# K in 8 KB pieces with the heads on alternate partitions, in a grouped-query attention kernel

## The chip, the cores and the metric

The kernel runs on one core of a Trainium2 chip. The metric is the device time of one execution in microseconds (us). The runs shown before the change have a median of 355.04 us (three runs, 353.94 to 355.42). The engines are named as in the profile: PE (matmuls; PEld are its weight loads), DVE (vector engine), ACT (activations), POOL, and SP, whose queue issues all transfers of this kernel.

## The reference

```python
B, Hq, Hkv, Sq, Sk, D = 16, 32, 8, 16, 2048, 128      # all bf16, normal * 0.05
k = jnp.repeat(k, Hq // Hkv, axis=1)
v = jnp.repeat(v, Hq // Hkv, axis=1)
scores = jnp.einsum("bhqd,bhkd->bhqk", q, k) * D ** -0.5
p = jax.nn.softmax(scores, axis=-1)
return jnp.einsum("bhqk,bhkd->bhqd", p, v)
```

There are 16 x 8 = 128 heads of K and V, each 2,048 keys of 128 values (512 KB). Four query heads of 16 rows share one of them, so each head of K meets 64 rows of Q.

## The kernel before

**Pairs.** Two heads of K (g = 0 and 1) make a pair p, and there are 64 pairs. Their 2 x 64 query rows fill the 128 partitions of S, P and O.

**Transfers (SP).** `load_k` (L143 to L151) brings the pair's K into one of six buffers `Kn`, `load_v` (L158) V into one of eight buffers `Vb`, `load_q` (L165) the Q of eight pairs, `store` (L170) a pair's output. SP's loop runs over t: K of pair t, Q when due, V of pair t - 4, the output of pair t - 17. A K load waits until the transposes of the pair that held its buffer are done, a V load until that pair's PV is done, a store until its output is written. In K and V of a head, partition a holds the 16 keys 16a to 16a + 15, 4 KB in one piece; a transfer of a pair thus has 256 pieces of 4 KB. The K of pair 0 comes as two transfers, one for each head, with a semaphore each.

**DVE.** For each pair it runs, in this order: the maximum of pair p (L281), the reciprocal of the row sums of pair p - 1 (L272), and the two transposes of K for pair p + 2 (L265). The transposes, one for each head, regard K as fp32 words (two bf16 side by side) and transpose blocks of 32 x 32 words, so that afterwards the partitions 32r to 32r + 31 hold the 32 words of a half of d, for the keys of row group r. The maximum reads the pair's 2,048 scores of S from PSUM, multiplies them by minus the scale, writes them to `Sneg` in SBUF as fp32 and takes the minimum along each row (`nbias`).

**PE.** Its order is written out in a list: S of pair p + 1 (L221), PV of pair p - 2 (L247), a part of the next Q's transposes if due (L204), the transposes of P of pair p (L236, in two halves of four). S has one buffer in PSUM, so S of the next pair waits for the maximum of this one. S of a pair is 32 matmuls, each over 32 partitions and 512 keys: four accumulations (the halves b of d and the two bf16 e of a word), four row groups r, two heads g. The moving operand is K, read one bf16 out of each fp32 word, with a step of 4 bytes:

```python
kt = KT[p % NKT][:, :, :].bitcast(BF16).rearrange("p g (t b x e) -> p g b e t x", t=J // 2, b=2, e=2)
```

**ACT.** It takes the exponential of `Sneg` into P (L310, with the row sums), copies the transposed P out of PSUM (L320), copies the transposed Q out of PSUM with a step of 128 bf16 in its input (L300), and scales the output of PV (L330). The exponential writes P in an order in which, after the transposes of P, the keys stand on the partitions on which V has them.

Of the kernel before, what the change touches and what calls it, by code (L numbers as in the profile page):

```python
# [7 lines left out]
BF16 = mybir.dt.bfloat16  # L8
F32 = mybir.dt.float32
I32 = mybir.dt.int32  # L10

NK = 6
NV = 8
NKT = 3
# [10 lines left out]
def bass_standalone__gqa_softmax__sampling_kernel(  # L25
# [11 lines left out]
    NP = G // 2  # L37
    J = Sk // 128
    assert J == 16 and NP % 8 == 0
    NQC = NP // 8  # L40
    scale = float(D) ** -0.5
# [5 lines left out]
    iota_t = sb("iota_t", [128, 128], I32)  # L47
    ident = sb("ident", [128, 128], BF16)
    ident4 = sb("ident4", [128, 128], F32)
    Kn = [sb(f"Kn{i}", [128, 2, J * 128], BF16) for i in range(NK)]  # L50
    Vb = [sb(f"Vb{i}", [128, 2, J, 128], BF16) for i in range(NV)]

    KT = [sb(f"KT{i}", [128, 2, J * 64], F32) for i in range(NKT)]
    Qn = [sb(f"Qn{i}", [128, 8, 128], BF16) for i in range(NQ)]

    QT = [sb(f"QT{i}", [128, 4, 1024], BF16) for i in range(2)]
# [27 lines left out]

    qf = q.rearrange("b h s d -> (b h s) d")
    of = out.rearrange("b h s d -> (b h s) d")
    kf = k.rearrange("b h s d -> (b h) (s d)").rearrange("g (a x) -> a g x", a=128)
    vf = v.rearrange("b h s d -> (b h) (s d)").rearrange("g (a x) -> a g x", a=128)  # L90


# [39 lines left out]
    with nc.Block() as block:  # L132
# [8 lines left out]
        @block.sync  # L141
        def _(sp):
            def load_k(p):  # L143
                s = p % NK
                if p >= NK:
                    sp.wait_ge(sem_kt, 2 * (p - NK) + 2)
                if p == 0:
                    for g in range(2):
                        sp.dma_start(Kn[s][:, g, :], kf[:, g, :]).then_inc(sem_k0[g], 16)  # L149
                else:  # L150
                    sp.dma_start(Kn[s][:, :, :], kf[:, 2 * p:2 * p + 2, :]).then_inc(sem_k[s], 16)  # L151

            def load_v(p):
                s = p % NV
                if p >= NV:
                    sp.wait_ge(sem_pv, p - NV + 1)
                dst = Vb[s][:, :, :, :].rearrange("a g j d -> a g (j d)")
                sp.dma_start(dst, vf[:, 2 * p:2 * p + 2, :]).then_inc(sem_v[s], 16)  # L158

            def load_q(c):  # L160
                s = c % NQ
                if c >= NQ:
                    sp.wait_ge(sem_st, last_q[c - NQ, 3] + 1)
                src = qf[1024 * c:1024 * (c + 1), :].rearrange("(a j) d -> a j d", j=8)
                sp.dma_start(Qn[s][:, :, :], src).then_inc(sem_q[s], 16)  # L165

            def store(p):
                s = p % NO
                sp.wait_ge(sem_nm, p + 1)
                sp.dma_start(of[128 * p:128 * (p + 1), :], Osb[s][:, :]).then_inc(sem_o[s], 16)  # L170

            for t in range(NP + SLAG + 1):
                if t < NP:
                    load_k(t)
                for c in range(NQC):
                    if t == max(0, 8 * c - QLEAD):
                        load_q(c)
                if 0 <= t - VLAG < NP:
                    load_v(t - VLAG)
                if 0 <= t - SLAG < NP:  # L180
                    store(t - SLAG)
            for s in range(NO):
                sp.wait_ge(sem_o[s], 16 * len(range(s, NP, NO)))

        @block.tensor
        def _(pe):
            pe.wait_ge(sem_id, 3)

            def free(u):
                if u >= NSTAGE:  # L190
                    pe.wait_ge(sem_ev, u - NSTAGE + 1)

            for op in pe_prog:
                if op[0] == "QT":
                    _, c, i, u = op
                    if i == 0:
                        pe.wait_ge(sem_q[c % NQ], 16 * (c // NQ + 1))
                    free(u)
                    dst = stage_ap(u).bitcast(BF16)
                    src = Qn[c % NQ][:, :, :].rearrange("p j (b c e) -> p j b e c", b=2, e=2)  # L200
                    b, e = divmod(i, 2)
                    for j in range(8):
                        for r in range(4):
                            ins = pe.transpose(dst[32 * r:32 * (r + 1), 128 * j:128 * (j + 1)], src[:, j, b, e, :], ident[:, :])  # L204
                    ins.then_inc(sem_st, 1)
                elif op[0] == "S":
                    _, p = op
                    pe.wait_ge(sem_kt, 2 * p + 2)
                    if p >= 1:
                        pe.wait_ge(sem_max, p)  # L210
                    c, i = divmod(p, 8)
                    if i == 0:
                        pe.wait_ge(sem_ev, last_q[c, 3] + 1)
                    kt = KT[p % NKT][:, :, :].bitcast(BF16).rearrange("p g (t b x e) -> p g b e t x", t=J // 2, b=2, e=2)
                    qt = QT[c % 2]
                    for acc in range(4):
                        b, e = divmod(acc, 2)
                        for r in range(4):
                            rows = slice(32 * r, 32 * (r + 1))
                            for g in range(2):  # L220
                                ins = pe.matmul(  # L221
                                    S_ps[64 * g:64 * (g + 1), 512 * r:512 * (r + 1)],
                                    qt[rows, acc, 128 * i + 64 * g:128 * i + 64 * (g + 1)],
                                    kt[rows, g, b, e, :, :],
                                    start=(acc == 0), stop=(acc == 3),
                                )
                    ins.then_inc(sem_s, 1)
                elif op[0] == "PT":
                    _, p, h, u = op
                    if h == 0:  # L230
                        pe.wait_ge(sem_exp, p + 1)
                    free(u)
                    dst = stage_ap(u)
                    for t in range(4):
                        x = 4 * h + t
                        ins = pe.transpose(dst[:, 128 * t:128 * (t + 1)], P[p % 2][:, 128 * x:128 * (x + 1)], ident4[:, :])  # L236
                    ins.then_inc(sem_st, 1)
                elif op[0] == "PV":
                    _, p = op
                    pe.wait_ge(sem_ev, last_p[p, 1] + 1)  # L240
                    pe.wait_ge(sem_v[p % NV], 16 * (p // NV + 1))
                    if p >= 1:
                        pe.wait_ge(sem_nm, p)
                    pt = PT[p % NPT][:, :, :].bitcast(BF16).rearrange("p t (q e) -> p t e q", e=2)
                    for j in range(J):
                        for g in range(2):
                            ins = pe.matmul(  # L247
                                O_ps[64 * g:64 * (g + 1), 0:128],
                                pt[:, j // 2, j % 2, 64 * g:64 * (g + 1)],
                                Vb[p % NV][:, g, j, :],  # L250
                                start=(j == 0), stop=(j == J - 1),
                                skip_group_check=True,
                            )
                    ins.then_inc(sem_pv, 1)

        @block.vector
        def _(dve):
            def kt(p, g):
                if p == 0:
                    dve.wait_ge(sem_k0[g], 16)  # L260
                else:
                    dve.wait_ge(sem_k[p % NK], 16 * (p // NK + (1 if p % NK else 0)))
                if p >= NKT:
                    dve.wait_ge(sem_s, p - NKT + 1)
                dve.transpose(  # L265
                    KT[p % NKT][:, g, :].rearrange("p (t b a e) -> p t e b a", t=J // 2, b=2, e=2),
                    Kn[p % NK][:, g, :].bitcast(F32).rearrange("p (t e b c) -> p t e b c", e=2, b=2, c=32),
                ).then_inc(sem_kt, 1)

            def recip(p):  # L270
# [1 line left out]
                dve.reciprocal(rrec[:, p:p + 1], rowsum[:, p:p + 1]).then_inc(sem_rec, 1)  # L272

            for p in range(2):
                for g in range(2):
                    kt(p, g)
            for p in range(NP):
                dve.wait_ge(sem_s, p + 1)
                if p >= 2:
                    dve.wait_ge(sem_exp, p - 1)  # L280
                dve.tensor_scalar(  # L281
                    Sneg[p % 2][:, :], S_ps[:, :], -scale, None,
                    op0=ALU.mult, op1=ALU.min, accum_out=nbias[:, p:p + 1],
                ).then_inc(sem_max, 1)
                if p >= 1:
                    recip(p - 1)
                if p + 2 < NP:
                    for g in range(2):
                        kt(p + 2, g)
            recip(NP - 1)  # L290

        @block.scalar
# [67 lines left out]
```

## Time and profile before

| | before |
|---|---|
| runs: median (lowest to highest) | 355.04 us (353.94 to 355.42) |
| the profiled execution | 354.38 us |
| its span, first to last instruction | 352.3 us |
| mean granted clock of PE | 0.935 |
| busy: DVE, ACT, PE | 296.3, 250.4, 246.5 us |
| bytes moved, mean rate over the span | 139.23 MB, 395 GB/s |
| packets of 4,096 B, of 2,048 B, of 256 B | 32,768, 1,024, 8,192 |
| K load, from issue to landing (median of 63) | 15.2 us |

A busy share is an average over the span: what counts is which wait ends last. A line of the profile's groups names line, engine, operation, output and input with their shapes and the count; then the busy time in us and the mean duration of one in ns; then the idle time of the engine just before them and what ended it. In the lists of waits stand total, count and longest. "issue" is time in which an engine waited for nothing that the profile shows. The trace also has a record of each DMA packet with its size and duration.

### The profile page before, as it was taken

To read this page: it belongs to the slowest core of one execution; us is meant where nothing else is said; L and a number is where in the kernel's file an instruction comes from. 1 tells how busy PE (TensorE), PEld (TensorE's weight loads), DVE (VectorE), ACT (ScalarE), POOL (GpSimd) and SP (SyncE) were. 2 spreads that over 40 slices of the span, in tenths; PEclk is the share of its full clock that TensorE was granted. 3 is DMA by queue.
4 is the path that set the end of the run, shared out by engine and by line. 5 is a ranking of instruction groups with operands and counts; after the bars stand their busy time and mean duration, and the time that the engine had idled before them with its cause. 6 is when DMAs were issued, how large, how long until landed. Compare 5 with 4: busy or idle time off the path is not lost.

```text
span 352.3 us, 12760 instructions
## 1 busy us (share of the span) xinstructions
PE 246.5 (70%) x5632; PEld 173.8 (49%) x5632; DVE 296.3 (84%) x320; ACT 250.4 (71%) x353; POOL 1.5 (0%) x7
## 2 busy tenths in 40 slices
PE   2587877667657596787776695776857778675783
PEld 2255554445436364564444373554544555454463
DVE  2899999878888798879988789887978898987860
ACT  2579788688577765768875876577757588865764
POOL 1000000000000000000000000000000000000000
PEclk9769999999899989889999989899989899998989
DMA  8999999999999999999999999999999999999982
GB/s 297 412 409 409 406 403 410 407 410 403 412 412 412 411 409 408 411 411 408 410 410 411 411 406 409 411 412 411 410 409 414 407 407 411 410 412 392 398 317 68
DMA packets 45254, 139.23 MB, mean 395 GB/s; under 512 B 11408, under 2 KB 11408, under 8 KB 45200
## 3 DMA queue, kind: packets, MB, share of 16 engines
q1 hardware_dynamic: 45200, 138.42, 99.1%
q8 instruction: 44, 0.72, 0.8%
q14 instruction: 10, 0.08, 0.1%
HBM read 136.31 MB, written 2.10 MB: 393 GB/s over the span
## 4 chain that ended last, share of the span: by engine, by line
PE 49%; issue 27%; DMA 12%; ACT 6%; DVE 4%; SPq 0%; ACTq 0%; DVEq 0%
PE O_ps L247 16%; PE ST_ps L236 15%; PE S_ps L221 14%; DMA Vb<-in_v_dram 10%; PE ST_ps L204 5%; ACT P L310 4%; DVE KT L265 3%; DMA Kn<-in_k_dram 2%; ACT PT L320 2%; DVE Sneg L281 1%; SPq L149 0%; ACT O L330 0%; SPq L165 0%; DVE rrec L272 0%; ACTq L329 0%
## 5 line engine op out<-in xcount | busy, mean ns | idle before, releaser
L265 DVE STREAM_TRANSPOSE KT<-Kn 128x1024 f32<-128x1024 f32 x128 | 151.6, 1223 | 34.9 <-DMA Kn<-in_k_dram 34.9
L281 DVE TENSOR_SCALAR_CACHE_REDUCE Sneg<-S_ps 128x2048 f32<-128x2048 f32 x64 | 144.7, 2261 | 11.9 <-PE S_ps L221 11.8
L310 ACT ACTIVATE P<-Sneg,nbias 128x2048 bf16<-128x2048 f32 x64 | 128.3, 2004 | 3.7 <-DVE Sneg L281 3.7
L247 PE MATMUL O_ps<-Vb,PT 128*64 128x128 bf16 x2048 | 75.8, 228 | 66.2 <-issue 61.2
L247 PEld LDWEIGHTS O_ps<-Vb,PT 128*64 128x64 bf16 x2048 | 65.2, 115 | 96.7 <-issue 83.4
L221 PE MATMUL S_ps<-KT,QT 32*64 32x512 bf16 x2048 | 78.1, 406 | 15.6 <-issue 7.6
L236 PE MATMUL ST_ps<-ident,P 128*128 128x128 f32 x512 | 78.8, 301 | 10.2 <-ACT P L310 8.1
L320 ACT ACTIVATE PT<-ST_ps 128x512 f32<-128x512 f32 x128 | 70.6, 597 | 18.6 <-PE ST_ps L236 18.5
L236 PEld LDWEIGHTS ST_ps<-ident,P 128*128 128x128 f32 x512 | 61.8, 153 | 20.2 <-ACT P L310 12.0
L330 ACT ACTIVATE O<-O_ps,rrec 128x128 bf16<-128x128 f32 x64 | 23.6, 368 | 59.9 <-PE O_ps L247 59.5
L221 PEld LDWEIGHTS S_ps<-KT,QT 32*64 32x64 bf16 x2048 | 29.4, 106 | 44.2 <-issue 31.4
L300 ACT ACTIVATE QT<-ST_ps 128x1024 bf16<-128x1024 bf16 x32 | 32.5, 1025 | 16.3 <-PE ST_ps L204 16.2
L204 PE MATMUL ST_ps<-ident,Qn 128*32 128x128 bf16 x1024 | 23.4, 241 | 10.6 <-DMA Qn<-in_q_dram 6.4
L204 PEld LDWEIGHTS ST_ps<-ident,Qn 128*32 128x32 bf16 x1024 | 17.4, 107 | 14.1 <-issue 11.8
L310 ACT ACTIVATION_READ_ACCUMULATOR P<-Sneg,nbias 128x1 f32 x64 | 13.0, 202 | 0.0
L272 DVE RECIPROCAL rrec<-rowsum 128x1 f32<-128x1 f32 x64 | 10.1, 158 | 2.3 <-ACT P L310 2.3
L281 DVE DVE_READ_ACCUMULATOR Sneg<-S_ps 128x1 f32 x64 | 5.3, 83 | 0.0
L300 ACT ACT_TABLE_LOAD x1 | 1.3, 1283 | 0.7 <-PEq L345 0.7
L138 POOL TENSOR_SCALAR ident<-iota_t 128x128 bf16<-128x128 int32 x1 | 0.5, 537 | 0.1
L139 POOL TENSOR_SCALAR ident<-iota_t 128x128 f32<-128x128 int32 x1 | 0.5, 528 | 0.0
L136 POOL IOTA iota_t<- 128x128 int32 x1 | 0.2, 235 | 0.4 <-POOLq L345 0.4
L345 POOL MEMSET const-bfloat16-1.0<- 128x1 bf16 x1 | 0.1, 102 | 0.0
(3 smaller groups left out, 0.3 us busy)
## 6 DMA issues: line engine op xcount, KB each, us to landing
Vb<-in_v_dram SPq DMA_DIRECT2D x64, 1024.0 KB, 16.3
Kn<-in_k_dram SPq DMA_DIRECT2D x63, 1024.0 KB, 15.2
Qn<-in_q_dram SPq DMA_DIRECT2D x8, 256.0 KB, 14.1
out_dram<-O SPq DMA_DIRECT2D x64, 32.0 KB, 13.7
Kn<-in_k_dram SPq DMA_DIRECT2D x2, 512.0 KB, 4.0
```

The lines of the kernel that those rows point to most:

```text
L138: gp.tensor_scalar(ident[:, :], iota_t[:, :], 0.0, None, op0=ALU.is_equal).then_inc(sem_id, 1)
L204: ins = pe.transpose(dst[32 * r:32 * (r + 1), 128 * j:128 * (j + 1)], src[:, j, b, e, :], ident[:, :])
L221: ins = pe.matmul(S_ps[64 * g:64 * (g + 1), 512 * r:512 * (r + 1)], qt[rows, acc, 128 * i + 64 * g:128 * i + 64 * (g + 1)], kt[rows, g, b, ...
L236: ins = pe.transpose(dst[:, 128 * t:128 * (t + 1)], P[p % 2][:, 128 * x:128 * (x + 1)], ident4[:, :])
L247: ins = pe.matmul(O_ps[64 * g:64 * (g + 1), 0:128], pt[:, j // 2, j % 2, 64 * g:64 * (g + 1)], Vb[p % NV][:, g, j, :], start=(j == 0), sto ...
L265: dve.transpose(KT[p % NKT][:, g, :].rearrange("p (t b a e) -> p t e b a", t=J // 2, b=2, e=2), Kn[p % NK][:, g, :].bitcast(F32).rearrange ...
L272: dve.reciprocal(rrec[:, p:p + 1], rowsum[:, p:p + 1]).then_inc(sem_rec, 1)
L281: dve.tensor_scalar(Sneg[p % 2][:, :], S_ps[:, :], -scale, None, op0=ALU.mult, op1=ALU.min, accum_out=nbias[:, p:p + 1],).then_inc(sem_max, 1)
L300: act.activation(QT[c % 2][:, i, :].rearrange("p (a j) -> p a j", j=8), stage_ap(u).bitcast(BF16).rearrange("p (j a) -> p a j", j=8), ACT. ...
L310: act.activation(P[p % 2][:, :].bitcast(BF16).rearrange("p (t r x) -> p t r x", t=8, r=4), Sneg[p % 2][:, :].rearrange("p (r t x) -> p t r ...
L320: act.activation(PT[p % NPT][:, 4 * h:4 * (h + 1), :].rearrange("p t q -> p (t q)"), stage_ap(u), ACT.Copy,).then_inc(sem_ev, 1)
L330: act.activation(Osb[p % NO][:, :], O_ps[:, 0:128], ACT.Copy, scale=rrec[:, p:p + 1]).then_inc(sem_nm, 1)
```

## The change

The layout of K in SBUF changes, and the patterns that read it; V, Q, the exponential, the transposes of P and PV stay as they are.

- K's source is cut into 64 pieces of 8 KB per head, 32 keys each. Piece a of head g goes to partition 2a + g: the heads alternate from partition to partition, and a transfer has 128 pieces of 8 KB. Its source pattern has 64 rows, two heads and 4,096 elements, its destination 128 partitions and 4,096 elements. For pair 0 there are two transfers, each with one half h (16 keys) of every piece.
- The two transposes of a pair take one half h each, of both heads. Behind them, both heads stand next to each other in the transposed row, and the transposes write 32 words side by side instead of one in two.
- S reads K for one head with a step of 4 bf16 (two words), 8 bytes. Its 512 columns are the same keys as before, in the order 16 x (key within the piece) + piece.
- The maximum reads S as (m, a, y) out of (m, y, a), with a = 16 and y = 4: four scores with a step of 16 fp32, then the next a. It writes `Sneg` in sequence, in the order that the exponential had before.

```diff
-    Kn = [sb(f"Kn{i}", [128, 2, J * 128], BF16) for i in range(NK)]
+    Kn = [sb(f"Kn{i}", [128, 2 * J * 128], BF16) for i in range(NK)]
-    KT = [sb(f"KT{i}", [128, 2, J * 64], F32) for i in range(NKT)]
+    KT = [sb(f"KT{i}", [128, 2 * J * 64], F32) for i in range(NKT)]
-    kf = k.rearrange("b h s d -> (b h) (s d)").rearrange("g (a x) -> a g x", a=128)
+    kf = k.rearrange("b h s d -> (b h s d)").rearrange("(p g a x) -> p a g x", p=NP, g=2, a=64)
...
-                    for g in range(2):
-                        sp.dma_start(Kn[s][:, g, :], kf[:, g, :]).then_inc(sem_k0[g], 16)
+                    for h in range(2):
+                        x = slice(2048 * h, 2048 * (h + 1))
+                        sp.dma_start(Kn[s][:, x], kf[p, :, :, x]).then_inc(sem_k0[h], 16)
                 else:
-                    sp.dma_start(Kn[s][:, :, :], kf[:, 2 * p:2 * p + 2, :]).then_inc(sem_k[s], 16)
+                    sp.dma_start(Kn[s][:, :], kf[p, :, :, :]).then_inc(sem_k[s], 16)
...
-                    kt = KT[p % NKT][:, :, :].bitcast(BF16).rearrange("p g (t b x e) -> p g b e t x", t=J // 2, b=2, e=2)
+                    kt = KT[p % NKT][:, :].bitcast(BF16).rearrange("p (b x g e) -> p g b e x", b=2, g=2, e=2)
...
-                                    kt[rows, g, b, e, :, :],
+                                    kt[rows, g, b, e, :],
...
-            def kt(p, g):
+            def kt(p, h):
                 if p == 0:
-                    dve.wait_ge(sem_k0[g], 16)
+                    dve.wait_ge(sem_k0[h], 16)
...
                 dve.transpose(
-                    KT[p % NKT][:, g, :].rearrange("p (t b a e) -> p t e b a", t=J // 2, b=2, e=2),
-                    Kn[p % NK][:, g, :].bitcast(F32).rearrange("p (t e b c) -> p t e b c", e=2, b=2, c=32),
+                    KT[p % NKT][:, :].rearrange("p (b t h e x) -> p h t e b x", b=2, h=2, t=J // 2, e=2)[:, h, :, :, :, :],
+                    Kn[p % NK][:, 2048 * h:2048 * (h + 1)].bitcast(F32).rearrange("p (t e b c) -> p t e b c", e=2, b=2, c=32),
                 ).then_inc(sem_kt, 1)
...
                 dve.tensor_scalar(
-                    Sneg[p % 2][:, :], S_ps[:, :], -scale, None,
+                    Sneg[p % 2][:, :].rearrange("p (m a y) -> p m a y", a=16, y=4),
+                    S_ps[:, :].rearrange("p (m y a) -> p m a y", a=16, y=4), -scale, None,
                     op0=ALU.mult, op1=ALU.min, accum_out=nbias[:, p:p + 1],
                 ).then_inc(sem_max, 1)
```

The callers of `kt` on DVE run over h instead of g.

More of the change, by code (lines that the diff above doesn't have):

```diff
@@ L274, in _ @@
             for p in range(2):
-                for g in range(2):
-                    kt(p, g)
+                for h in range(2):
+                    kt(p, h)
             for p in range(NP):
@@ L287, in _ @@
                 if p + 2 < NP:
-                    for g in range(2):
-                        kt(p + 2, g)
+                    for h in range(2):
+                        kt(p + 2, h)
             recip(NP - 1)
```

## The prediction

> **What bounds the kernel now.** I read the page's 40 slices first, and in them the two lines of the DMA.
>
> ```profile
> DMA  8999999999999999999999999999999999999982
> GB/s 297 412 409 409 406 403 410 407 410 403 412 412 412 411 409 408 411 411 408 410 410 411 411 406 409 411 412 411 410 409 414 407 407 411 410 412 392 398 317 68
> DMA packets 45254, 139.23 MB, mean 395 GB/s; under 512 B 11408, under 2 KB 11408, under 8 KB 45200
> q1 hardware_dynamic: 45200, 138.42, 99.1%
> ```
>
> The 16 DMA engines are full from the second slice to the 38th, at a flat rate near 410 GB/s. No compute engine is flat. The next view is the table of stretches: its columns are the stretch and its length, the busy time of PE, PEld, DVE, ACT and POOL, the granted clock, the DMA share and GB/s.
>
> ```profile
> 64.00:330.00 266.00, 189.09 (x4336) 133.33 (x4328) 230.01 (x250) 192.96 (x273) 0.00 (x0) 0.94 1.03 409
> ```
>
> In the steady stretch the DMA share is 1.03 (packet records overlap by some 3%), DVE has 230 of 266 us. Then the waits of DVE, and those of the queue that issues the transfers:
>
> ```profile
> DVE KT L265 <- DMA Kn<-in_k_dram: 34.9, 43, 4.3
> DVE Sneg L281 <- PE S_ps L221: 11.8, 9, 2.6
> ...
> SPq L158 <- PE O_ps L247: 59.2, 34, 3.7
> SPq L151 <- DVE KT L265: 52.2, 48, 3.2
> ```
>
> DVE waits for K, in 43 of 64 pairs. SP waits for free buffers, but a K load lands 15.2 us after its issue (median), about three pairs of heads later, so the engines' queues never run dry: those waits bound nothing. One pair moves 139.23 MB / 64 = 2.18 MB, which at 409 GB/s is 5.3 us. What DVE would need is in the timeline where it did not wait:
>
> ```profile
> 156.01 2.29 DVE L281 TENSOR_SCALAR_CACHE_REDUCE Sneg<-S_ps 128x2048 f32<-128x2048 f32 x1 [1.72 <-PE S_ps L221]
> ...
> 158.30 2.35 DVE L265 STREAM_TRANSPOSE KT<-Kn 128x1024 f32<-128x1024 f32 x2
> ...
> 160.58 2.25 DVE L281 TENSOR_SCALAR_CACHE_REDUCE Sneg<-S_ps 128x2048 f32<-128x2048 f32 x1
> ```
>
> From 156.01 to 160.58 is 4.57 us per pair. The first such maximum starts at 12.59 us and the last at 340.65, 5.21 us apart on average; DVE alone could do it in 63 x 4.57 = 287.9 us instead of 328.1. It has 40 us to spare, 0.64 us per pair. The kernel is bound by its transfers; DVE is next, PE (246.5 us busy) and ACT (250.4) behind it.
>
> **The change, part by part.** *The K transfers.* In 63 of 64 pairs, 256 pieces of 4 KB become 128 of 8 KB; over 16 engines that is 8 packets fewer per engine and pair, 63 x 8 = 504 in all, for the same bytes. The packet records of the trace price a packet: 4 B take 9 ns, 256 B 18, 2,048 B 84, 4,096 B 159 (medians; mean 162.4). From 2,048 to 4,096 B is 75 ns, so 84 - 75 = 9 ns of each packet do not depend on its size. A packet of 8 KB should take 159 + 150 = 309 ns where two of 4 KB take 318. Not all of the 9 ns need be time lost, for the records overlap: one engine's packets of a pair add up to 32 x 161 + 8 x 18 + 86 and some 75 ns for semaphores and instructions, 5.46 us, against 5.32 us (2.18 MB at 409 GB/s): 0.14 us over some 44 packets, 3 ns each. So a packet saved is worth between 9 - 3 = 6 ns and 9 ns: 3.0 to 4.5 us over 504. I take 7 ns, on the careful side: 3.5 us. Ends beyond it: the trace has 16 packets of 8 KB, on another queue; those in the middle of the run took 309 to 338 ns, with one of 444. At 309 the saving is the 4.5 us again; at 338 each costs 20 ns more than two of 4 KB, and 504 of them lose 10 us. I take the fit, since most of the clean ones lie within 16 ns of it, and keep +10 us for the rivals.
>
> [...]
>
> *The two K loads of pair 0* stay 4 KB pieces, 512 KB each: nothing. *Issues:* 201 as before, at the same places in SP's program, and no wait is added or moved.
>
> *The transposes (L265).* As many, as long (1,024 elements, 1,223 ns), their writes now step 4 bytes instead of 8. Between this row and the maximum (2,048 elements, 2,261 ns, written without a step) one element costs 1,038 / 1,024 = 1.01 ns, so the step of 8 costs nothing today, and its removal gives nothing. Zero, no end on either side that matters.
>
> *S on PE (L221).* 32 matmuls of 512 columns now read K with a step of 8 bytes instead of 4. No row shows a step of 8. Lower bound 0, as nothing is read less; upper bound twice the time of the 32, 1.11 us more per pair (71 us more PE, 317 of 352). I take 0: the step of 4 already runs 32 of them in 1.11 us. The cover is the transposes: S of the next pair starts when the maximum has ended, and DVE then has 2.35 + 0.24 us of other work before it needs it. Even a doubled 2.22 us fits; it shows only where PE stands still for "issue" (7.6 us before L221, 61.2 before L247), and once in the tail.
>
> *The maximum (L281)* reads S with an inner step of 16 fp32, 64 bytes, in runs of four. No DVE row reads PSUM so. The nearest rows are ACT's, which also read PSUM:
>
> ```profile
> L320 ACT ACTIVATE PT<-ST_ps 128x512 f32<-128x512 f32 x128 | 70.6, 597 | 18.6 <-PE ST_ps L236 18.5
> L300 ACT ACTIVATE QT<-ST_ps 128x1024 bf16<-128x1024 bf16 x32 | 32.5, 1025 | 16.3 <-PE ST_ps L204 16.2
> L281 DVE TENSOR_SCALAR_CACHE_REDUCE Sneg<-S_ps 128x2048 f32<-128x2048 f32 x64 | 144.7, 2261 | 11.9 <-PE S_ps L221 11.8
> ```
>
> L320 reads without a step, L300 with an inner step of 256 bytes in runs of eight. The 512 elements more cost 428 ns, 0.84 ns each; 597 - 512 x 0.84 leaves 169 ns fixed, and so does 1025 - 1024 x 0.84. A step of 256 bytes out of PSUM costs ACT nothing. DVE takes 1.01 ns per element, more slowly than ACT, so I take 0. The other end is one element in two cycles: 2,048 x 1.01 = 2.08 us more per pair. Its output is still written without a step, so the exponential (L310) is untouched.
>
> [...]
>
> *The tail.* The last transposes start at 333.36 us and the program ends 18.9 us later, through S, maximum, exponential, PV and store. This stays; it moves forward with the last K.
>
> **Sum.** The profiled execution took 354.38 us, of which 352.3 span: 354.38 - 3.5 = 350.9. The median of the runs is 0.66 us above the profiled one, so 351.5 us. DVE would then wait 3.5 us less for K, and still some 31.
>
> **The rivals.** *DVE pays for the step (chance 0.14).* The engine that is next becomes the bound. At two cycles per element its pair takes 4.57 + 2.08 = 6.65 us, the last maximum starts at 12.59 + 63 x 6.65 = 431.5 instead of 340.65 and takes 2.1 us longer: 355 + 91 + 2 = 448 us. It decides from 0.64 us per maximum, that is from 2.9 us instead of 2.26; below that the transfers hide it. For it speaks only that DVE's row is missing; against it the two rows of ACT.
>
> *The transfers of K get slower, not faster (0.12).* Their source is now 64 rows by two heads against 128 partitions, where V and today's K have 128 rows on both sides, and no row shows how such a transfer is split over 16 engines. At 338 ns per packet it is 355 + 10 = 365 us; if K's half of the traffic went at half its rate, 2.6 us more per pair, 355 + 64 x 2.6 = 521 us.
>
> *PE gets late (0.05).* S takes up to 1.11 us more, and the instruction fetches (44 packets of 16 KB, 1.07 us each, on a queue of their own beside longer K packets) may take longer. PE's order is S, PV, transposes of P; where an "issue" stall of 1.5 to 3 us falls into the pair, the 2.6 us cover is gone. A loss of 0.3 us on half the pairs beyond the spare time gives about 365 us; zero is as well possible.
>
> *No change (0.17).* The fixed part of a packet is hidden by the overlap, or the rate is held elsewhere at 410 GB/s: 353.5 to 356.5 us. That K does not land in larger pieces is within this case; the profile would then still show 32,768 packets of 4 KB.
>
> **How the numbers follow.** The forecast has 0.52, with its own range 349.5 to 353.2 (a gain of 1.8 to 5.5 us; the fit's 3.0 to 4.5 and the spread of 1.5 us among the runs shown). A measurement of this kernel tells 0.5%, 1.8 us, from no change. Faster is 0.52, same 0.17, slower 0.14 + 0.12 + 0.05 = 0.31. From 349 us the range takes in the forecast and no change (0.69), and to reach 0.8 it must go into the mild slower cases: to 370 us it holds PE late and the K packets at 338 ns, some 0.12 more. The doublings lie outside.
>
> **What would show it.** Right: 16,640 packets of 4 KB and 8,064 of 8 KB at about 309 ns, GB/s in the steady stretch near 414 instead of 409, L281 at 2,261 ns and L265 at 1,223, S's 32 matmuls still within 1.2 us, and waits of L265 for K near 31 us. Wrong: L281 above 2.9 us with no wait for K left and a DVE near 100%; or a DMA share still full at a lower rate; or 8 KB packets above 320 ns.

## The result and the profile after

The changed kernel takes 351.42 us (median of five runs, 350.64 to 351.87) against 354.86 us; the ratio is 0.9899, with a 95% interval of 0.9863 to 0.9934. In a second comparison, later, it was 0.9914 (0.9883 to 0.9946). The forecast was 351.5 us. The profiled execution took 351.62 us, of which 349.8 span.

From the page's slices, the lines of the DMA, and the first queue:

```profile
DMA  7999999999999999999999999999999999999972
GB/s 266 420 420 414 409 416 409 411 416 411 413 417 418 415 414 415 415 414 415 416 414 416 417 409 414 416 416 415 415 412 419 417 412 416 413 415 416 386 286 51
DMA packets 37190, 139.23 MB, mean 398 GB/s; under 512 B 11408, under 2 KB 11408, under 8 KB 29072
q1 hardware_dynamic: 37136, 138.42, 98.1%
```

The bytes are the same, the packets 8,064 fewer (63 pairs x 128), the engines as full as before (a DMA share of 1.02 for 1.03 in the steady stretch), the rate some 5 GB/s higher in nearly every slice of the middle. The packet records have 16,640 of 4,096 B and 8,064 of 8,192 B for K and V; those of 8 KB, all of K, take 309 ns (median, and also the quarter points), those of 4 KB 159 as before. The steady stretch of the table by stretches:

```profile
64.00:330.00 266.00, 227.78 (x4440) 130.84 (x4424) 235.76 (x255) 197.08 (x279) 0.00 (x0) 0.99 1.02 414
```

PE, the first column behind the length, has 228 us where it had 189; the last column is 414 GB/s for 409. The granted clock is 0.99 for 0.94, but the time does not come from it: with S at 4 bytes (below) it is 0.95 again, and the time is the same (350.8 us). The groups that the change touches, first two of them before and then three after:

```profile
L265 DVE STREAM_TRANSPOSE KT<-Kn 128x1024 f32<-128x1024 f32 x128 | 151.6, 1223 | 34.9 <-DMA Kn<-in_k_dram 34.9
L221 PE MATMUL S_ps<-KT,QT 32*64 32x512 bf16 x2048 | 78.1, 406 | 15.6 <-issue 7.6 <-DVE Sneg L281 6.2 <-DVE KT L265 1.5
```

```profile
L267 DVE STREAM_TRANSPOSE KT<-Kn 128x1024 f32<-128x1024 f32 x128 | 151.3, 1220 | 22.9 <-DMA Kn<-in_k_dram 22.9
L284 DVE TENSOR_SCALAR_CACHE_REDUCE Sneg<-S_ps 128x2048 f32<-128x2048 f32 x64 | 145.3, 2270 | 20.3 <-PE S_ps L223 19.8
L223 PE MATMUL S_ps<-KT,QT 32*64 32x512 bf16 x2048 | 131.8, 625 | 18.0 <-DVE Sneg L284 9.8
```

What DVE waited for after the change, from the list of waits:

```profile
DVE KT L267 <- DMA Kn<-in_k_dram: 22.9, 30, 5.1
DVE Sneg L284 <- PE S_ps L223: 19.8, 17, 2.3
```

(L267, L284 and L223 are L265, L281 and L221 of before.) The transposes and the maximum are as long as they were. S is not: one matmul takes 625 ns instead of 406 (means), and the 32 of a pair take 2.00 us instead of 1.11. DVE's waits, for K and for S together, fell from 46.7 to 42.7 us, about what the kernel gained; but K's part fell by 12 us and S's rose by 8.

The timeline shows how the longer S lies beside DVE's transposes:

```profile
157.04 2.35 DVE L267 STREAM_TRANSPOSE KT<-Kn 128x1024 f32<-128x1024 f32 x2
158.71 2.01 PE L223 MATMUL S_ps<-KT,QT 32*64 32x512 bf16 x32
160.77 2.29 DVE L284 TENSOR_SCALAR_CACHE_REDUCE Sneg<-S_ps 128x2048 f32<-128x2048 f32 x1 [1.38 <-PE S_ps L223]
```

Here S started 1.7 us later than the transposes, and DVE waited 1.38 us for it. Where S starts on time, the transposes cover it.

### The profile page after: what moved, and what is told of

The parts are those of the page before. It is cut to its first block, busy times and chain, and to the rows that moved or that the text cites. A ratio compares the mean times of both kernels' runs of the same rounds, so it can differ in the third digit from the quotient of the medians.

```text
span 349.8 us, 12760 instructions
## 1 busy us (share of the span) xinstructions
PE 288.3 (82%) x5632; PEld 166.7 (48%) x5632; DVE 296.2 (85%) x320; ACT 251.2 (72%) x353; POOL 1.5 (0%) x7
## 4 chain that ended last, share of the span: by engine, by line
PE 60%; issue 22%; DVE 12%; ACT 3%; DMA 1%; SPq 0%; DVEq 0%; ACTq 0%
PE S_ps L223 28%; PE O_ps L249 14%; PE ST_ps L238 13%; DVE KT L267 9%; PE ST_ps L206 5%; DVE Sneg L284 3%; DMA Qn<-in_q_dram 1%; ACT P L314 1%; ACT QT L304 1%; ACT PT L324 1%; SPq L151 0%; DVE rrec L274 0%; ACT O L334 0%; DVEq L266 0%; DVEq L282 0%
## 5 line engine op out<-in xcount | busy, mean ns | idle before, releaser
L267 DVE STREAM_TRANSPOSE KT<-Kn 128x1024 f32<-128x1024 f32 x128 | 151.3, 1220 | 22.9 <-DMA Kn<-in_k_dram 22.9
L284 DVE TENSOR_SCALAR_CACHE_REDUCE Sneg<-S_ps 128x2048 f32<-128x2048 f32 x64 | 145.3, 2270 | 20.3 <-PE S_ps L223 19.8
L223 PE MATMUL S_ps<-KT,QT 32*64 32x512 bf16 x2048 | 131.8, 625 | 18.0 <-DVE Sneg L284 9.8
L249 PEld LDWEIGHTS O_ps<-Vb,PT 128*64 128x64 bf16 x2048 | 61.8, 112 | 80.5 <-issue 68.8
L249 PE MATMUL O_ps<-Vb,PT 128*64 128x128 bf16 x2048 | 72.3, 223 | 25.3 <-issue 24.5
L324 ACT ACTIVATE PT<-ST_ps 128x512 f32<-128x512 f32 x128 | 69.9, 596 | 12.9 <-PE ST_ps L238 12.8
L238 PE MATMUL ST_ps<-ident,P 128*128 128x128 f32 x512 | 72.6, 284 | 5.1 <-issue 2.9
L223 PEld LDWEIGHTS S_ps<-KT,QT 32*64 32x64 bf16 x2048 | 31.8, 113 | 71.8 <-issue 69.1
L238 PEld LDWEIGHTS ST_ps<-ident,P 128*128 128x128 f32 x512 | 56.4, 143 | 14.4 <-ACT P L314 4.7
L304 ACT ACTIVATE QT<-ST_ps 128x1024 bf16<-128x1024 bf16 x32 | 32.5, 1025 | 15.8 <-PE ST_ps L206 15.8
L206 PE MATMUL ST_ps<-ident,Qn 128*32 128x128 bf16 x1024 | 22.5, 235 | 9.9 <-DMA Qn<-in_q_dram 7.4
L206 PEld LDWEIGHTS ST_ps<-ident,Qn 128*32 128x32 bf16 x1024 | 16.7, 104 | 13.1 <-issue 10.5
L284 DVE DVE_READ_ACCUMULATOR Sneg<-S_ps 128x1 f32 x64 | 5.3, 83 | 0.0
```

Of the source, the lines that this page charges most:

```text
L223: ins = pe.matmul(S_ps[64 * g:64 * (g + 1), 512 * r:512 * (r + 1)], qt[rows, acc, 128 * i + 64 * g:128 * i + 64 * (g + 1)], kt[rows, g, b, ...
L249: ins = pe.matmul(O_ps[64 * g:64 * (g + 1), 0:128], pt[:, j // 2, j % 2, 64 * g:64 * (g + 1)], Vb[p % NV][:, g, j, :], start=(j == 0), sto ...
L267: dve.transpose(KT[p % NKT][:, :].rearrange("p (b t h e x) -> p h t e b x", b=2, h=2, t=J // 2, e=2)[:, h, :, :, :, :], Kn[p % NK][:, 2048 ...
L284: dve.tensor_scalar(Sneg[p % 2][:, :].rearrange("p (m a y) -> p m a y", a=16, y=4), S_ps[:, :].rearrange("p (m y a) -> p m a y", a=16, y=4 ...
L304: act.activation(QT[c % 2][:, i, :].rearrange("p (a j) -> p a j", j=8), stage_ap(u).bitcast(BF16).rearrange("p (j a) -> p a j", j=8), ACT. ...
L324: act.activation(PT[p % NPT][:, 4 * h:4 * (h + 1), :].rearrange("p t q -> p (t q)"), stage_ap(u), ACT.Copy,).then_inc(sem_ev, 1)
```

## The experiments

All have the kernel before on the same chip beside them: 354.1 us in the first group (17 runs: S at 4 bytes, S at 8 bytes before, V in 8 KB, K in 2 KB), 354.2 in the second (15: S at 16 bytes, V in 8 KB with S at 4 bytes, the heads apart, and the changed kernel again, 351.67 us), 354.3 in the third (13: S at 2 bytes, and the last run of the heads apart).

### S with a step of 4 bytes again

```diff
-kt = KT[p % NKT][:, :].bitcast(BF16).rearrange("p (b x g e) -> p g b e x", b=2, g=2, e=2)
+kt = KT[p % NKT][:, :].bitcast(BF16).rearrange("p (b g x e) -> p g b e x", b=2, g=2, e=2)
```

> The changed kernel, but S reads the transposed K with a step of 4 bytes, as before the change; its words are then those of both heads, so S is of mixed keys, with the same number of matmuls, columns and waits. Theory A (the transfers set the pace, S's doubled time is hidden): S's 32 matmuls go back from 2.00 us to about 1.1 us, PE busy from 288 to about 247 us, DVE's waits for S from 20 to about 12 us, and the time stays within 1.5 us of the changed kernel's 351.4, at most 1 us of it from the tail. Rival B (S's longer time has eaten a part of the saving): 347 to 349 us. A second rival, that S did not get slower through the step but through the two heads lying in one row: S stays at 2.00 us.

Measured: 350.8 us, ratio 0.9912 (0.9882 to 0.9941), the same as with the step of 8. First the group of S, then DVE's waits:

```profile
L223 PE MATMUL S_ps<-KT,QT 32*64 32x512 bf16 x2048 | 80.2, 416 | 17.0 <-DVE Sneg L284 7.7 <-issue 7.5 <-DVE KT L267 1.5
```

```profile
DVE KT L267 <- DMA Kn<-in_k_dram: 33.4, 45, 5.0
DVE Sneg L284 <- PE S_ps L223: 8.8, 9, 1.9
```

S's 32 matmuls are back at 1.11 us although both heads still lie in one row: it was the step. DVE waits 11 us less for S, and 10.5 us more for K, which comes no sooner. Nearly all of the time that S had taken was hidden under the transfers (what shows of it in the tail, below 1 us, comes further down); rival B's 347 to 349 us did not come.

### S with a step of 8 bytes in the kernel before

```diff
-kt = KT[p % NKT][:, :, :].bitcast(BF16).rearrange("p g (t b x e) -> p g b e t x", t=J // 2, b=2, e=2)
+kt = KT[p % NKT][:, :, :].rearrange("p g w -> p (g w)").bitcast(BF16).rearrange("p (b x g e) -> p g b e x", b=2, g=2, e=2)
...
-kt[rows, g, b, e, :, :],
+kt[rows, g, b, e, :],
```

> The kernel before, with one edit: S reads K with a step of 8 bytes, out of the same tile of both heads (so of mixed keys, the same number of columns). K and V still come in 4 KB pieces. Theory A: S's 32 matmuls take 2.0 us instead of 1.11 us, PE busy goes from 246 to about 290 us, and the time stays at that of before within 1 us, for the transfers cover it. Rival B: the time grows by 1.5 us or more.

Measured: 354.77 us, ratio 1.0002 (0.9974 to 1.0031). S's matmuls take 625 ns, 2.00 us for 32. DVE's waits:

```profile
DVE Sneg L281 <- PE S_ps L221: 25.3, 19, 2.3
DVE KT L265 <- DMA Kn<-in_k_dram: 21.3, 26, 4.3
```

Those for S rise from 11.8 us and those for K fall from 34.9: the same exchange in the other direction. The time moves by less than the interval can tell, some 1 us.

### S with a step of 2 and of 16 bytes

```diff
-"p (b x g e) -> p g b e x"
+"p (b g e x) -> p g b e x"     # 2 bytes
+"p (x b g e) -> p g b e x"     # 16 bytes
```

> The changed kernel, but S reads the transposed K without a step (2 bytes; of mixed words, the same number of columns). [...] Time 350 to 352 us either way.

> The changed kernel, but S reads the transposed K with a step of 16 bytes (of mixed keys and words, the same number of columns). From 4 to 8 bytes S went from 1.11 to 2.00 us. [...] If anything above 4 bytes costs the same, S stays at 2.0 us and the time at 351.4.

Measured: without a step 374 ns per matmul (median), 1.07 us for 32, and 350.64 us in one run. With 16 bytes 1,073 ns, 3.78 us for 32 (not the 2.0 us of a cost that is the same for every step above 4 bytes), and 430.86 us, ratio 1.2145 (1.2092 to 1.2198). From the kernel with 16 bytes, the group of S, the wait for it, and its place in the timeline, one after the other:

```profile
L223 PE MATMUL S_ps<-KT,QT 32*64 32x512 bf16 x2048 | 243.9, 1072 | 19.6 <-DVE Sneg L284 14.8 <-issue 3.0 <-ACT QT L304 1.8
```

```profile
DVE Sneg L284 <- PE S_ps L223: 114.6, 64, 4.1
```

```profile
159.00 2.35 DVE L267 STREAM_TRANSPOSE KT<-Kn 128x1024 f32<-128x1024 f32 x2
159.16 3.78 PE L223 MATMUL S_ps<-KT,QT 32*64 32x512 bf16 x32
163.02 2.29 DVE L284 TENSOR_SCALAR_CACHE_REDUCE Sneg<-S_ps 128x2048 f32<-128x2048 f32 x1 [1.67 <-PE S_ps L223]
```

S starts with the transposes and outlives them; DVE waits for S in all 64 pairs. A pair takes 6.3 us here (156.71 to 163.02), more than the 5.3 us that the transfers need (2.18 MB at 414 GB/s). The cover is gone, as the two lengths say: S of 3.78 us does not fit into the 2.6 us, S of 2.00 us does. No step in between was run.

The four steps together, for 32 matmuls: 1.07 us at 2 bytes, 1.11 at 4, 2.00 at 8, 3.78 at 16. The shortest, median and longest of the single matmuls in ns, in the same order:

```profile
L223 PE MATMUL S_ps<-KT,QT x2048: 371/374/632, 12.6 to 336.1; 32*64 32x512 bf16 x187
L223 PE MATMUL S_ps<-KT,QT x2048: 380/383/632, 12.5 to 336.1; 32*64 32x512 bf16 x187
L223 PE MATMUL S_ps<-KT,QT x2048: 603/626/647, 12.4 to 336.2; 32*64 32x512 bf16 x187
L223 PE MATMUL S_ps<-KT,QT x2048: 1052/1073/1120, 12.6 to 416.0; 32*64 32x512 bf16 x187
```

From 8 to 16 bytes one matmul gets 447 ns longer, and the 32 get 1.78 us longer, four times as much. So, as an estimate from these two numbers, about eight run side by side (four row groups, two heads), and the 32 count as 4 x 512 = 2,048 columns one after another. That makes 0.87 ns more a column from 8 to 16 bytes, 0.43 ns more from 4 to 8 (0.89 us for the 32), and 0.02 ns more from 2 to 4 (0.04 us). From 4 bytes on the numbers fit, as an estimate, a column of 0.43 ns at 4 bytes that takes twice as long with each doubling of the step, and some 0.22 us for the 32 that do not change.

### V in 8 KB pieces as well

```diff
-vf = v.rearrange("b h s d -> (b h) (s d)").rearrange("g (a x) -> a g x", a=128)
+vf = v.rearrange("b h s d -> (b h s d)").rearrange("(p g a x) -> p a g x", p=NP, g=2, a=64)
...
-dst = Vb[s][:, :, :, :].rearrange("a g j d -> a g (j d)")
+dst = Vb[s][:, :, :, :].rearrange("a g j d -> a (g j d)")
-sp.dma_start(dst, vf[:, 2 * p:2 * p + 2, :]).then_inc(sem_v[s], 16)
+sp.dma_start(dst, vf[p, :, :, :]).then_inc(sem_v[s], 16)
```

> The changed kernel, with V too in 8 KB pieces, cut as K is; V then lies on other partitions than P expects, so P meets the wrong rows of V, with the same work. Theory A (a fixed cost of 6 to 9 ns for each packet is what was saved): 64 x 8 = 512 packets fewer per engine, another 3 to 4.5 us: about 347.8 us, the rate of the steady stretch from 414 to about 419 GB/s, if DVE and PE do not come to bind first (DVE's waits for K would fall from 23 to below 20 us). Rival C (the saving came from the order in which the heads are read, or from K's place in the stream, not from the number of packets): 351.4 us, no change. If DVE and PE bind, the rate stays near 414 GB/s and K's waits go to zero.

Measured: 348.82 us, ratio 0.9861 (0.9827 to 0.9894). The steady stretch:

```profile
64.00:330.00 266.00, 231.16 (x4475) 132.19 (x4461) 237.97 (x258) 199.32 (x281) 0.00 (x0) 0.97 1.02 419
```

The rate went where theory A put it, 419 GB/s, and the packets of 8 KB are 309 ns each again. The time fell further: by 1.3 to 1.9 us going by the ratios (0.0038 to 0.0053 of the kernel before), by 2.9 us going by the medians on the same chip (351.67 to 348.82). Either is short of the 3 to 4.5 us expected. To see whether S's longer time had kept the rest:

> V in 8 KB pieces as well (P then meets the wrong rows of V), and S reading with a step of 4 bytes (mixed keys). With V in 8 KB pieces alone the rate rose by another 5 GB/s to 419, 1.2% or 4 us, but the time fell by only 1.3 to 2.6 us. Theory E (what is missing was lost to S's longer time, mostly in the tail): now 346.5 to 347.8 us, DVE's waits for S near 10 us instead of 21. Rival F (it is lost elsewhere, or the difference is within the spread of the runs): 348.8 us again.

Measured: 349.04 us, ratio 0.9847 (0.9801 to 0.9892): no different. S is not the reason. The six runs of this kernel go from 347.46 to 350.62 us, and the one with the profile is the fastest of them (span 345.5 us, 3.9 us below that of the kernel with K alone in 8 KB and S at 4 bytes).

The traces show that the transfers gave nearly all of it. The last transposes start at 327.17 us with V in 8 KB pieces as well, where they start at 330.08 with K alone; with S at 4 bytes it is 327.04 against 330.49. That is 2.9 and 3.5 us earlier, against the 3 to 4.5 expected. What the profile with S at 8 bytes lost lies behind them: 21.1 us to the end instead of 19.7, and 1.2 of these 1.4 us come after the last ACT instruction. How much of the gain the median of the runs keeps is within their spread of some 3 us.

### K in 2 KB pieces in the kernel before

```diff
-sp.dma_start(Kn[s][:, :, :], kf[:, 2 * p:2 * p + 2, :]).then_inc(sem_k[s], 16)
+for h in range(2):
+    x = slice(1024 * h, 1024 * (h + 1))
+    sp.dma_start(Kn[s][:, :, x], kf[:, 2 * p:2 * p + 2, x]).then_inc(sem_k[s], 16)
...
-dve.wait_ge(sem_k[p % NK], 16 * (p // NK + (1 if p % NK else 0)))
+dve.wait_ge(sem_k[p % NK], 32 * (p // NK + (1 if p % NK else 0)))
```

> The kernel before, with K of pairs 1 to 63 in two transfers, each with one half of every piece: 512 pieces of 2 KB per pair instead of 256 of 4 KB, and one transfer more. Theory A: 63 x 16 = 1,008 data packets more per engine (and 63 semaphore packets) at 6 to 9 ns: 6.4 to 9.6 us slower than before, 361 to 364.5 us, the steady rate near 400 GB/s instead of 409. Rival C: within 1 us of before.

Measured: 362.21 us, ratio 1.0232 (1.0207 to 1.0257), 8.2 us more than before. The steady stretch:

```profile
64.00:330.00 266.00, 188.55 (x4270) 131.86 (x4263) 226.55 (x245) 189.37 (x268) 0.00 (x0) 0.92 1.04 399
```

8.2 us over 1,008 packets per engine are 8.1 ns each (7.3 to 9.0 by the interval). The second transfer of each pair also adds 63 packets of 4 B per engine, for its semaphore; counted with them it is 7.6 ns. The 3.6 us of the change over 504 packets are 7.1 ns (4.6 to 9.6), and by the second comparison 6.0 (3.8 to 8.2). The order of the heads did not change here, the number of packets did. DVE waits 46.8 us for K.

### The heads apart in SBUF, for a step of 4 bytes

```diff
-KT[p % NKT][:, :].rearrange("p (b t h e x) -> p h t e b x", b=2, h=2, t=J // 2, e=2)[:, h, :, :, :, :],
-Kn[p % NK][:, 2048 * h:2048 * (h + 1)].bitcast(F32).rearrange("p (t e b c) -> p t e b c", e=2, b=2, c=32),
+KT[p % NKT][:, 1024 * h:1024 * (h + 1)].rearrange("p (g t h y) -> p h t y g", g=2, h=2, y=32),
+Kn[p % NK][:, :].bitcast(F32).rearrange("p (n b c) -> p b n c", b=2, c=32)[:, h, :, :],
```

S reads with `"p (b g x e) -> p g b e x"`, and for pair 0 each transpose waits for both transfers.

> The changed kernel with the same 8 KB pieces, in which each transpose takes one half of d of both heads and writes the two heads to two places 2 KB apart, alternating from word to word, so that S can read each head with a step of 4 bytes. Same keys, same result. Theory A: S is back at 1.1 us, the transposes stay at 1,220 ns if DVE's writes do not care for the step; then the time is that of the changed kernel, 350.3 to 351.9 us, since S's time was hidden. Rival D (DVE's writes pay for alternating between two places): the transposes take up to 2.2 us; above 1.5 us each DVE binds, and at 2.2 us the time is about 64 x 2 - 40 = 88 us more, 440 us.

Measured: 404.05 us, ratio 1.1392 (1.135 to 1.1435). The group of the transposes, and PE's longest wait for DVE:

```profile
L268 DVE STREAM_TRANSPOSE KT<-Kn 128x1024 f32<-128x1024 f32 x128 | 250.2, 2063 | 6.7 <-DMA Kn<-in_k_dram 6.7
```

```profile
PE S_ps L223 <- DVE Sneg L285: 111.3, 56, 2.9
```

S is at 1.11 us again, but a transpose takes 2,046 ns (median) instead of 1,224, and now PE waits for DVE. DVE is busy for 266.0 of the 266 us between 64 and 330, and the rate falls to 374 GB/s. Rival D named what costs the time; its 440 us were too high, mostly because two transposes together take 3.91 us and not 4.4: DVE's pair is 6.0 us in the timeline, and 64 x (6.0 - 5.2) is 51 us. The edit had also changed the order in which K is read, so one more run keeps that order of reading and writes side by side (S reads with 8 bytes again):

```diff
-KT[p % NKT][:, 1024 * h:1024 * (h + 1)].rearrange("p (g t h y) -> p h t y g", g=2, h=2, y=32),
+KT[p % NKT][:, 1024 * h:1024 * (h + 1)].rearrange("p (t h y) -> p h t y", h=2, y=64),
```

> The changed kernel, same layout of K behind the transposes, but each transpose takes one half of d of both heads' 32 keys (it reads 32 words, skips 32) instead of 16 keys with both halves, and writes 64 words side by side. With the heads written to two places 2 KB apart the transposes took 2,046 ns instead of 1,220; that edit also read K in this way. Theory G (the writes that alternate between two places cost): transposes at 1,220 ns and the time of the changed kernel, 350.6 to 352 us. Rival H (the reads that skip cost): about 2,000 ns and 404 us.

Measured: 351.25 us, ratio 0.992 (0.9897 to 0.9942). The shortest, median and longest transposes, with the heads apart and in this run:

```profile
L268 DVE STREAM_TRANSPOSE KT<-Kn x128: 1940/2046/2320, 6.7 to 383.0; 128x1024 f32<-128x1024 f32 x128
L268 DVE STREAM_TRANSPOSE KT<-Kn x128: 1194/1212/1246, 6.8 to 331.1; 128x1024 f32<-128x1024 f32 x128
```

The reads that skip cost nothing (1,212 ns, and 1,224 in the changed kernel, medians); the writes that alternate between two places do (2,046).

## Why the prediction was right

**What bounds the kernel.** Transfers did, and do. Four kernels show it, with the same bytes in fewer and fewer packets: K in 2 KB pieces 399 GB/s, all in 4 KB 409, K in 8 KB 414, K and V in 8 KB 419. And two show it from the other side: S's time nearly doubled or halved, with the transfers left as they are, moves the time by less than the 1 us that the runs can tell. The 8 KB pieces also change the order in which the heads are read, and no run changes that order alone. The price from the 2 KB pieces, where the order stays, already gives 3.8 to 4.1 us for the 504 packets, so nothing of the gain is left for the order to explain.

**The price of a packet** was put at 7 ns, from 6 to 9; the two comparisons of the change give 7.1 and 6.0, with some 2 ns to either side, and the 2 KB pieces 7.6 to 8.1. The fit from the rows of 2 and 4 KB said 309 ns for 8 KB, and 309 it is. The rows of 309 to 338 ns from the other queue, which had to serve as the far end, were not like K's.

**The maximum's step of 64 bytes** costs nothing: 2,270 ns against 2,261, and the 9 ns more are not its own: with the same pattern and S at 4 bytes it takes 2,263, and with the old pattern and S at 8 bytes 2,269. (The four scores of a run are two neighbouring keys from each half of a piece: the columns of S stand in the order 16 x (4t + 2h + e) + piece, where the key within the piece is 16h + 2t + e, and not in the plain order of the keys.) ACT's rows were the right neighbours: 1,025 ns for 1,024 elements of bf16 in steps of 256 bytes (L300) is no more per element than 597 ns for 512 of fp32 without a step (L320). That both leave 169 ns fixed adds nothing to this, since the 0.84 ns are the difference of the same two rows.

**S's step of 8 bytes** is the term that was mis-sized: "I take 0" has to read 0.89 us per pair, near the upper end of 1.11. The argument for 0, that with a step of 4 the 32 already run in 1.11 us, says nothing about 8, and no row did. The cover that the prediction named held it: DVE has 2.6 us of other work, S of 2.00 us fits, and what came through is what the prediction had named too, a late S here and there and the tail. That the cover has an end, the step of 16 bytes showed.

**DVE's waits for K** were expected near 31 us and came out at 22.9. The sum of its waits fell by 4.0 us, as the transfers gave; the split moved, because S took 8 us of it.

**The tail** was to stay at 18.9 us; it is 19.7 (last transposes at 330.08, end at 349.8). From the timeline after the change, and the last transposes with S at 4 bytes:

```profile
327.65 2.29 DVE L284 TENSOR_SCALAR_CACHE_REDUCE Sneg<-S_ps 128x2048 f32<-128x2048 f32 x1 [0.66 <-PE S_ps L223]
330.08 2.37 DVE L267 STREAM_TRANSPOSE KT<-Kn 128x1024 f32<-128x1024 f32 x2
336.88 2.29 DVE L284 TENSOR_SCALAR_CACHE_REDUCE Sneg<-S_ps 128x2048 f32<-128x2048 f32 x1 [2.17 <-PE S_ps L223]
```

```profile
330.49 2.37 DVE L267 STREAM_TRANSPOSE KT<-Kn 128x1024 f32<-128x1024 f32 x2 [0.44 <-DMA Kn<-in_k_dram]
```

The last transposes no longer wait for K but for the maximum in front of them, which had waited 0.66 us for S, and S in the tail is itself longer: the last maximum waits 2.17 us for it, and 1.39 with S at 4 bytes. There the tail is 18.9 us (330.49 to 349.4). So the 0.8 us are S's, as far as single profiles tell; the stretch behind the last ACT instruction alone differs by 0.5 us between these two.

**The number came closer than its terms.** The sum was 350.9 us for the profiled execution, which took 351.62: the transfers gave 3.3 us (last transposes at 330.08 instead of 333.36), the tail took 0.8 back, and the span fell by 2.5. The prediction then added 0.66 us, because the median had stood that far above the profiled run; after the change it stands 0.2 below. The two misses cancel, and that is luck. The medians fell by 3.4 us in the first comparison and by 2.6 in the second.

**The rivals.** DVE did not become the bound. The transfer with 64 rows on one side and 128 on the other ran at the rate of the others: 309 ns for 8 KB, where two of V's packets of 4 KB take 318. PE got later, as that rival said: S took 0.89 us more of the 1.11 that it allowed, and but for the tail that stayed inside the time that was to spare. No change is out: the interval of the ratio ends at 0.9934, and K lands in pieces of 8 KB.

## What to carry to other kernels

With full DMA engines (a DMA share of 1.02 to 1.04) a piece here costs its bytes and some 6 to 8 ns more, so the larger pieces of K paid a little and as predicted (medians 2.6 and 3.4 us lower for 504 packets fewer per engine), and the records of two sizes gave the price (9 ns here, a little high). The layout that made the pieces larger moved its cost into a pattern behind it (S's 32 matmuls from 1.11 to 2.00 us): list each reader and writer, and for each the engine that waits and the work that hides it, for a hidden cost is a cost as soon as the cover is shorter (S at 2.00 us cost less than 1 us, at 3.78 us it cost a fifth). A free step on one engine says nothing about another engine, nor about the next larger step: here 64 bytes cost DVE's maximum nothing (2,263 ns against 2,261), and S took 0.04 us more at 4 bytes than at 2, but 0.89 us more at 8 than at 4.

## What was not expected of the hardware

The 32 matmuls of S, with K as their moving operand in bf16 and 32 partitions each, take hardly longer at a step of 4 bytes than at 2, and 1.8 times as long at 8 and 3.4 times as long at 16 as at 4 (1.07, 1.11, 2.00, 3.78 us). No such matmul over all 128 partitions was tried. DVE's transpose of 128 x 1,024 fp32 words takes 1,220 ns when it writes words side by side and 1,223 when it writes one in two, and 2,063 ns when successive words go to two places 2 KB apart (means); DVE's maximum, reading fp32 from PSUM in steps of 64 bytes in runs of four, is as fast as without a step (2,263 against 2,261 ns). And PE was granted more of its clock where S went more slowly: a mean of 0.96 to 0.99 in every run with S at 8 or 16 bytes, and 0.86 to 0.96 in every run with S at 2 or 4.
